# Third layer's input weights: seven forms made in block 0 of stage two instead of in stage one

## The chip, the cores and the metric

One core of a Trainium2 chip. The time is the device time of one execution in microseconds (us); the lower, the better.

## What is computed

Three layers, all in float32. `q`, `k`, `v` are 8 x 8 heads x 576 x 64, `p` is 32 packed queries a head; `moe_w_in` and `moe2_w_in` are 512 x 2048, `moe_w_out` and `moe2_w_out` 2048 x 512 (passed as 64-bit floats and converted on the chip).

```python
def sm_attn(qq, kk, vv):
    s = scale * np.matmul(qq, kk.transpose(0, 1, 3, 2))
    s = s - np.max(s, axis=-1, keepdims=True)
    a = np.exp(s)
    a = a / (np.sum(a, axis=-1, keepdims=True) + 1e-09)
    return np.matmul(a, vv)
p_packed = sm_attn(p, k, v)
x = sm_attn(q, p_packed, p_packed)     # then 4608 tokens x 512
h = x @ moe_w_in;  x = (h * np.cos(h)) @ moe_w_out
h = x @ moe2_w_in
sp = np.where(h > 20.0, h, np.log1p(np.exp(np.minimum(h, 20.0))))
out = (h * np.tanh(sp)) @ moe2_w_out
```

## The kernel before

Every product is made from a high and a low part: a float32 matrix is split into `hi` (a cast on ScalarE) and `lo = x - hi` (a subtraction, mostly on GpSimd), and `mm3` issues three matmuls for one.

**Stage one** makes the attention and the second layer. It runs over n = 0 to 258. Step n issues `l1(n)` (6 matmuls of 288 columns: one of 16 blocks of features for one of 16 tiles of tokens), background work listed for that step, and `l2(n - 3)` (12 matmuls into four accumulators). Between them lies the chain of the step: `chain_first` and `chain_cos` (lines 793 to 803, ScalarE and VectorE) and `chain_split` (line 810 on ScalarE, 813 on GpSimd). The attention of later tiles, the folded weights of the second layer and the third layer's weights are background work, put into the tables `bg_pe`, `bg_ew`, `bg_ld` at given steps. A scheduler that simulates the program fixes each engine's order; each engine then runs its list strictly in that order.

**Stage two** is the third layer, in five blocks of 512, 448, 448, 448 and 448 tokens. Each of its products is done by a seven-product scheme (Strassen's, in Winograd's form) on 2 x 2 blocks. For the first product the weight `moe2_w_in` (`w2i`) is cut into eight units p; each has seven *forms*: its four quadrants, and three sums of them. Per block and p, `product` makes seven products x = 0 to 6 (6 matmuls each), and `sub` puts items of the second product (3 matmuls each) between them. The weight tile of product m is asked for by `ws_load`, five products ahead, since the tag `tmp` has 5 buffers.

**Where the forms come from.** Before, stage one makes all of them. `U_AT` places 16 units at steps 44, 68, ... (`w2i_unit`) and 56, 80, ... (`w2o_unit`, the same for `moe2_w_out`), one each 12 steps. A unit loads two raw tiles of 512 KB (two buffers of tag `raw`), converts them in place (`raw_conv`: lines 548 on ScalarE, 549 and 550 on VectorE), and in the steps +3 to +10 runs the list of `form`: four sums of quadrants on GpSimd (line 569) and seven splits (line 562 on ScalarE, 563 on GpSimd), each followed by a store of 256 KB to memory (line 632 for `w2i`, 598 for `w2o`). Stage two loads each form again in every block (line 532).

All DMAs are issued by SyncE (SP), one queue in order.

Of the kernel before, what the change touches and what calls it, by code (L numbers as in the profile page):

```python
# [8 lines left out]
F32 = mybir.dt.float32  # L9
F32R = mybir.dt.float32r  # L10
I32 = mybir.dt.int32
# [62 lines left out]
T_BUFS = 6  # L74
T_AHEAD = 6
P_AHEAD = 3
U_AT = tuple(44 + 12 * j for j in range(16))
SCALE = 1.0 / math.sqrt(D)
EPS = 1e-9
TWO_PI = 2.0 * math.pi  # L80
# [4 lines left out]
def build(tc, q, k, v, p, w1i, w1o, w2i, w2o, out):  # L85
    nc = tc.nc
    ctx = ExitStack()
    with ctx:
# [6 lines left out]
        def nm(s):  # L95
            cnt[0] += 1
            return f"{s}_{cnt[0]}"
# [422 lines left out]
            return conv(w1o[128 * ft : 128 * ft + 128, :], [128, 512], dst, None)  # L520

        WST = {}

        WS = {}
        NQ = 56 * 5

        def ws_load(m):
            if m >= NQ:
                return
            p, k = divmod(m % 56, 7)  # L530
            w = WS[m] = tp.tile([128, 2, 2, 128], F32R, tag="tmp", bufs=TMP_BUFS, name=nm("ws"))
            nc.sync.dma_start(w.bitcast(F32), WST[(p, K3[k])])

        TST = {}

        def raw_load(raw, parts):
            def f():
                r = tp.tile([128, 512, 2], I32, tag="raw", bufs=2, name=nm("raw"))
                for dst, src in parts(r):
                    nc.sync.dma_start(dst, src)  # L540
                raw.append(r)

            return f
# [32 lines left out]
        def w2o_unit(p):  # L576
            raw = []

            def parts(x):
                def f(r):  # L580
                    src = w2o[256 * p + 128 * x : 256 * p + 128 * x + 128, :].bitcast(I32)
                    for h in range(2):
                        for c in range(2):
                            o = 256 * h + 128 * c
                            yield (
                                r[:, o : o + 128].rearrange("q (a j) t -> q a (j t)", a=4),
                                src[:, 512 * h : 512 * h + 512].rearrange("q (a c y) -> q c a y", a=4, c=2)[:, c],
                            )

                return f  # L590

            def quad(raw, xh):
                x, h = divmod(xh, 2)
                return raw[x][:, 256 * h : 256 * h + 256, 1].bitcast(F32)

            def store(k, w):
                d = TST[(p, k)] = dram.tile([128, 512], F32, name=nm("tst"))
                nc.sync.dma_start(d, w.bitcast(F32).rearrange("p x a f -> p (x a f)"))

            SB = ALU.subtract  # L600
            steps = (
                ((0, 1), None),
                ((2, 2), None),
                (0, 1, 0, SB),
                ((0, 5), None),
                ((3, 3), None),
                (1, 3, 1, SB),
                ((1, 7), None),
                (3, 3, 0, SB),
                ((3, 6), None),  # L610
                (2, 2, 3, SB),
                ((2, 4), None),
            )
            return [raw_load(raw, parts(0)), raw_load(raw, parts(1))], form(raw, quad, store, steps)

        def w2i_unit(p):
            raw = []

            def parts(c):
                def f(r):  # L620
                    src = w2i[256 * c : 256 * c + 256, 256 * p : 256 * p + 256].rearrange("(a p) f -> p a f", p=128)
                    yield r.rearrange("p (a f) t -> p a (f t)", f=256), src.bitcast(I32)

                return f

            def quad(raw, ch):
                c, h = divmod(ch, 2)
                return raw[c].rearrange("p (a f) t -> p a f t", f=256)[:, :, 128 * h : 128 * h + 128, 1].bitcast(F32)

            def store(k, w):  # L630
                d = WST[(p, k)] = dram.tile([128, 2, 2, 128], F32, name=nm("wst"))
                nc.sync.dma_start(d, w.bitcast(F32))

            SB = ALU.subtract
            steps = (
                ((0, 0), None),
                ((2, 1), None),
                (0, 0, 1, SB),
                ((0, 3), None),
                ((3, 4), None),  # L640
                (1, 1, 3, ALU.add),
                ((1, 5), None),
                (3, 3, 0, SB),
                ((3, 2), None),
                (2, 2, 3, SB),
                ((2, 6), None),
            )
            return [raw_load(raw, parts(0)), raw_load(raw, parts(1))], form(raw, quad, store, steps)

# [15 lines left out]
        def at_ew(n, f):  # L665
            bg_ew.setdefault(n, []).append(f)

        def at_ld(n, f):
            bg_ld.setdefault(n, []).append(f)
# [8 lines left out]
        def place(stages, steps, off=0):  # L678
            for (pe, ew), n in zip(stages, steps):
                if off:  # L680
                    pe, ew = pe and hp(pe, off), ew and hp(ew, off)
                if pe is not None:
                    at_pe(n, pe)
                if ew is not None:
                    at_ew(n, ew)
# [52 lines left out]
                at_ew(n, ew)  # L738

        for j, n in enumerate(U_AT):  # L740
            loads, steps = (w2i_unit if j % 2 == 0 else w2o_unit)(j // 2)
            for f in loads:
                at_ld(n, f)
            for i, f in steps:
                at_ew(n + i, f)

        for pair in range(3):
            n0 = 64 * pair
# [16 lines left out]
        for t in range(1, NT):  # L765
            n = Q_N[t - 1]
            loads, stages = q_unit(t)
            at_ld(n - (Q_LD if t > 3 else Q_LD0), after_w(loads))
            place(stages, [n + i for i in (Q_SUB if t > 3 else Q_SUB0)])
        for m in range(TMP_BUFS):  # L770
            at_ld(COMB + 3 + m, lambda m=m: ws_load(m))

        for n in range(PRO - 4, 0):
            run_bg(bg_pe, n)
# [87 lines left out]
        def x_sums(i, a):  # L862
            def f():
                n = N_BLK[i]
                b1, b2 = raws[(i, a)]
                b11, b12, b21, b22 = b1[:, :n], b1[:, n:], b2[:, :n], b2[:, n:]
                t2, t3, t4 = [ld_tile([128, 512])[:, :n] for _ in range(3)]
                nc.vector.tensor_tensor(t3, b22, b12, ALU.subtract)
                nc.vector.tensor_tensor(b12, b12, b11, ALU.subtract)
                nc.vector.tensor_tensor(t2, b22, b12, ALU.subtract)  # L870
                nc.vector.tensor_tensor(t4, b21, t2, ALU.subtract)
                raws[(i, a)] = (b11, b21, t2, t3, t4, b12, b22)

            return f
# [53 lines left out]
        def product(i, p, x, ps, n, first=True):  # L928
            m = 56 * i + 7 * p + x
            w, src = WS.pop(m), X[(i, K3[x])]  # L930
            for a in range(2):
                mm3(ps, w[:, 0, a], w[:, 1, a], src[:, a, 0, :n], src[:, a, 1, :n], first and a == 0, a == 1, not first)
            ws_load(m + TMP_BUFS)

        def split(hl, src, n, eng):
            nc.scalar.copy(hl[:, 0, :n], src)  # L936
# [222 lines left out]
```

## Time and profile before

| | us |
|---|---|
| median of 3 runs | 1581.95 |
| lowest, highest | 1576.72, 1590.94 |
| the profiled execution | 1587.78 |
| its span, first to last instruction | 1585.8 |
| TensorE busy | 1492.7 (94%) |
| VectorE, ScalarE, GpSimd busy | 1093.4, 895.0, 672.3 |

The profile is of one execution, 5.8 us above the median of the runs. A matmul's end is modelled, so "busy" for TensorE hides gaps that are shorter than the modelled overlap of two matmuls. In the names, PE is TensorE, PEld its weight load, DVE VectorE, ACT ScalarE, POOL GpSimd, SP or SPq SyncE and its DMA queue. "acc<-gh,wo" is `l2`, "ps<-aT,wab" `l1`, "ps<-wab,ws" a product of stage two, "acc<-gh,T" an item of its second product.

### The profile page before, as it was taken

What the parts mean: (1) busy time and instruction counts of PE and PEld (TensorE: products, weight loads), DVE (VectorE), ACT (ScalarE), POOL (GpSimd) and SP (SyncE); (2) the same over time, 40 slices, a digit from 0 to 9 for tenths busy, and PEclk for the clock granted to TensorE, in tenths of its full rate; (3) what the DMA queues carried; (4) which work ended last, traced back from release to release, by engine and by line L of the source; (5) the groups of instructions that cost most, each with busy time, mean ns of one, the idle gap of its engine ahead of it and who ended that gap; (6) DMA issues with size and microseconds to landing.
All of it is one profiled execution on the core that took longest, in us unless ns stands there. A gap on an engine that the chain in (4) does not pass through costs nothing.

```text
span 1585.8 us, 28624 instructions
## 1 busy us (share of the span) xinstructions
PE 1492.7 (94%) x9728; PEld 1302.5 (82%) x9728; DVE 1093.4 (69%) x2044; ACT 895.0 (56%) x1844; POOL 672.3 (42%) x682
## 2 busy tenths in 40 slices
PE   3778999999999999998999999999999999999997
PEld 1566778788987898788999888889999899999986
DVE  4885667677766776778764557687567658756656
ACT  3675767677766776766764345435444533543343
POOL 0451346357653665647843025225223521532142
PEclk9889999999999999999999999999999999999999
DMA  9888676557556556543323668788778878777955
GB/s 290 276 214 206 175 186 191 170 146 205 154 158 180 168 163 164 175 123 109 120 68 119 198 197 248 204 231 263 232 214 258 253 213 229 240 215 207 262 150 169
DMA packets 250833, 307.05 MB, mean 194 GB/s; under 512 B 104768, under 2 KB 129856, under 8 KB 250688
## 3 DMA queue, kind: packets, MB, share of 16 engines
q1 hardware_dynamic: 250688, 305.22, 66.6%
q8 instruction: 78, 1.28, 0.3%
q14 instruction: 67, 0.55, 0.1%
HBM read 252.71 MB, written 52.43 MB: 192 GB/s over the span
## 4 chain that ended last, share of the span: by engine, by line
PE 70%; DMA 9%; DVE 7%; ACT 4%; issue 4%; POOL 4%; SPq 1%; DVEq 0%; POOLq 0%; ACTq 0%
PE acc L142 12%; PE acc L143 12%; PE acc L144 12%; PE ps L142 10%; PE ps L143 10%; PE ps L144 10%; PE ps L488 2%; POOL wt L563 2%; DMA raw<-in_moe_w_out_dram 2%; DMA raw<-in_moe_w_in_dram 1%; DVE r L796 1%; DMA kr<-in_k_dram 1%; DVE r L795 1%; DMA kr<-in_q_dram 1%; POOL raw L569 1%
## 5 line engine op out<-in xcount | busy, mean ns | idle before, releaser
L813 POOL TENSOR_TENSOR gh<-r,gh 128x288 fp32r<-128x288 f32 x256 | 216.7, 853 | 286.3 <-ACT gh L810 204.1
L937 POOL TENSOR_TENSOR gh<-t,gh 128x448 fp32r<-128x448 f32 (+1 forms) x120 | 155.2, 1298 | 427.9 <-ACT gh L936 427.9
L143 PE MATMUL acc<-gh,wo 128*128 128x288 f32 x1024 | 301.7, 301 | 1.8 <-POOL gh L813 1.6
L144 PE MATMUL acc<-gh,wo 128*128 128x288 f32 x1024 | 298.2, 298 | 0.0
L142 PE MATMUL acc<-gh,wo 128*128 128x288 f32 x1024 | 276.7, 305 | 6.7 <-ACT gh L810 5.9
L142 PEld LDWEIGHTS acc<-gh,wo 128*128 128x128 f32 x1024 | 182.3, 191 | 41.7 <-issue 16.5
L143 PE MATMUL acc<-gh,T 128*128 128x448 f32 (+1 forms) x560 | 209.6, 374 | 1.3 <-DVE gh L937 1.3
L144 PE MATMUL acc<-gh,T 128*128 128x448 f32 (+1 forms) x560 | 208.9, 374 | 0.0
L143 PE MATMUL ps<-wab,ws 128*128 128x448 f32 (+1 forms) x560 | 208.2, 372 | 0.0
L142 PE MATMUL ps<-wab,ws 128*128 128x448 f32 (+1 forms) x560 | 206.7, 372 | 1.3 <-DMA ws<-wst 1.2
L143 PEld LDWEIGHTS acc<-gh,wo 128*128 128x128 f32 x1024 | 194.1, 190 | 15.8 <-issue 10.1
L144 PE MATMUL ps<-wab,ws 128*128 128x448 f32 (+1 forms) x560 | 206.9, 372 | 0.0
L144 PEld LDWEIGHTS acc<-gh,wo 128*128 128x128 f32 x1024 | 194.2, 190 | 4.1 <-issue 4.0
L937 DVE TENSOR_TENSOR gh<-wo,gh 128x448 fp32r<-128x448 f32 (+1 forms) x160 | 128.8, 810 | 95.4 <-ACT gh L936 94.6
L142 PE MATMUL acc<-gh,T 128*128 128x448 f32 (+1 forms) x560 | 186.5, 375 | 3.2 <-ACT gh L936 3.2
L142 PE MATMUL ps<-aT,wab 128*128 128x288 f32 x512 | 161.1, 315 | 28.2 <-DVE r L803 20.1
L802 ACT ACTIVATE r<-r,halfpi 128x288 f32<-128x288 f32 x256 | 136.2, 535 | 84.4 <-DVE r L796 82.8
L803 DVE TENSOR_TENSOR r<-r,ps 128x288 f32<-128x288 f32 x256 | 114.4, 448 | 69.1 <-ACT r L802 68.1
L143 PE MATMUL ps<-aT,wab 128*128 128x288 f32 x512 | 153.1, 299 | 0.0
L144 PE MATMUL ps<-aT,wab 128*128 128x288 f32 x512 | 152.4, 298 | 0.0
L795 DVE SCALAR_TENSOR_TENSOR r<-ki,ps 128x288 f32<-128x288 int32 x256 | 113.5, 446 | 55.0 <-ACT ki L793 35.7
L793 ACT ACTIVATE ki<-ps,quarter 128x288 int32<-128x288 f32 x256 | 124.0, 495 | 47.5 <-PE ps L144 36.8
(150 smaller groups left out, 2968.5 us busy)
## 6 DMA issues: line engine op xcount, KB each, us to landing
ws<-wst SPq DMA_DIRECT2D x280, 256.0 KB, 3.0
T<-tst SPq DMA_DIRECT2D x280, 256.0 KB, 2.9
kr<-in_k_dram SPq DMA_DIRECT2D x64, 272.0 KB, 5.4
ld<-ws SPq DMA_DIRECT2D x64, 256.0 KB, 3.7
kr<-in_q_dram SPq DMA_DIRECT2D x60, 272.0 KB, 5.3
wst<-wt SPq DMA_DIRECT2D x56, 256.0 KB, 2.7
tst<-wt SPq DMA_DIRECT2D x56, 256.0 KB, 2.2
x2d<-xo SPq DMA_DIRECT2D x64, 144.0 KB, 1.8
```

The costliest lines, as they stand in the source:

```text
L142: nc.tensor.matmul(ps, l0, r0, start=first, stop=False, skip_group_check=more)
L143: nc.tensor.matmul(ps, l0, r1, start=False, stop=False, skip_group_check=more)
L144: nc.tensor.matmul(ps, l1, r0, start=False, stop=last, skip_group_check=more)
L488: return nc.tensor.matmul(st[b][32 * l : 32 * l + 32], PK[(b, g)][r : r + 64, 32 * l : 32 * l + 32], ms[h // 2]["m"][r : r + 64], start=Tr ...
L563: nc.gpsimd.tensor_tensor(lo, src, hi, ALU.subtract)
L569: nc.gpsimd.tensor_tensor(quad(raw, a), quad(raw, b), quad(raw, c), d)
L793: nc.scalar.activation(ki, st["h"], AF.Identity, bias=quarter, scale=1.0 / TWO_PI)
L795: nc.vector.scalar_tensor_tensor(r, ki, -TWO_PI, st["h"], ALU.mult, ALU.add)
L802: nc.scalar.activation(g, g, AF.Sin, bias=halfpi, scale=1.0)
L803: nc.vector.tensor_tensor(g, g, st["h"], ALU.mult)
L813: nc.gpsimd.tensor_tensor(gh[:, 1], st["g"], gh[:, 0], ALU.subtract)
L937: eng.tensor_tensor(hl[:, 1, :n], src, hl[:, 0, :n], ALU.subtract)
```

## The change

`w2i_unit` is gone. `U_AT` now places only the eight `w2o` units, at steps 83 to 220, every 19 or 20 steps. The raw halves of `w2i`, 16 of 512 KB, are placed by `I_AT` at steps 44, 53, 63, 73 and then two behind each `w2o` unit. Each is loaded and converted by `conv` (steps c1 to c3: one operation on ScalarE, two on VectorE, through two `tmp` buffers), and the converted words are stored, 256 KB each, without being summed or split.

In block 0 of stage two, for each unit p: `comb_load` reads the two converted tiles back into two `ld` buffers, `comb_sums` makes the three sums with four operations on VectorE into two more `ld` buffers (of six), and `ws_load` makes each of the 56 weight tiles by a cast on ScalarE and a subtraction on GpSimd, and stores it for blocks 1 to 4. These load the forms as before. The first unit's work and its first five tiles stand in the last steps of stage one (240 to 247). Since `ld` is now in use in block 0, `x_sums` of block 1 writes into buffers of the tags `V` and `o`.

```diff
--- before.py
+++ after.py
@@ -74,7 +74,9 @@
 T_BUFS = 6
 T_AHEAD = 6
 P_AHEAD = 3
-U_AT = tuple(44 + 12 * j for j in range(16))
+U_AT = tuple(83 + 98 * j // 5 for j in range(8))
+I_AT = (44, 53, 63, 73) + tuple(83 + 98 * (j // 2) // 5 + 13 + 3 * (j % 2) for j in range(12))
+I_LAG = 2
 SCALE = 1.0 / math.sqrt(D)
 EPS = 1e-9
 TWO_PI = 2.0 * math.pi
@@ -520,6 +522,30 @@
             return conv(w1o[128 * ft : 128 * ft + 128, :], [128, 512], dst, None)
 
         WST = {}
+        w2s = {}
+
+        def pre2(key, src, shape):
+            return conv(src, shape, None, lambda d: w2s.__setitem__(key, d))
+
+        CB = {}
+
+        def comb_load(p):
+            CB[p] = []
+            for c in range(2):
+                r = ld_tile([128, 512])
+                nc.sync.dma_start(r, w2s[(p, c)])
+                CB[p].append(r.rearrange("p (a f) -> p a f", f=256))
+
+        def comb_sums(p):
+            c0, c1 = CB[p]
+            a11, a21, a12, a22 = c0[:, :, :128], c0[:, :, 128:], c1[:, :, :128], c1[:, :, 128:]
+            u, v = [ld_tile([128, 512]).rearrange("p (x a f) -> p x a f", x=2, a=2) for _ in range(2)]
+            nc.vector.tensor_tensor(u[:, 0], a21, a22, ALU.add)
+            nc.vector.tensor_tensor(u[:, 1], u[:, 0], a11, ALU.subtract)
+            nc.vector.tensor_tensor(v[:, 0], a11, a21, ALU.subtract)
+            nc.vector.tensor_tensor(v[:, 1], a12, u[:, 1], ALU.subtract)
+            CB[p] = (a11, a12, u[:, 1], v[:, 0], a22, u[:, 0], v[:, 1])
+
 
         WS = {}
         NQ = 56 * 5
@@ -529,7 +555,13 @@
                 return
             p, k = divmod(m % 56, 7)
             w = WS[m] = tp.tile([128, 2, 2, 128], F32R, tag="tmp", bufs=TMP_BUFS, name=nm("ws"))
-            nc.sync.dma_start(w.bitcast(F32), WST[(p, K3[k])])
+            if m < 56:
+                nc.scalar.copy(w[:, 0], CB[p][K3[k]])
+                nc.gpsimd.tensor_tensor(w[:, 1], CB[p][K3[k]], w[:, 0], ALU.subtract)
+                d = WST[(p, K3[k])] = dram.tile([128, 2, 2, 128], F32, name=nm("wst"))
+                nc.sync.dma_start(d, w.bitcast(F32))
+            else:
+                nc.sync.dma_start(w.bitcast(F32), WST[(p, K3[k])])
 
         TST = {}
 
@@ -610,40 +642,6 @@
                 ((3, 6), None),
                 (2, 2, 3, SB),
                 ((2, 4), None),
-            )
-            return [raw_load(raw, parts(0)), raw_load(raw, parts(1))], form(raw, quad, store, steps)
-
-        def w2i_unit(p):
...
             return [raw_load(raw, parts(0)), raw_load(raw, parts(1))], form(raw, quad, store, steps)
 
@@ -738,11 +736,18 @@
                 at_ew(n, ew)
 
         for j, n in enumerate(U_AT):
-            loads, steps = (w2i_unit if j % 2 == 0 else w2o_unit)(j // 2)
+            loads, steps = w2o_unit(j)
             for f in loads:
                 at_ld(n, f)
             for i, f in steps:
                 at_ew(n + i, f)
+        for j, n in enumerate(I_AT):
+            w, c = divmod(j, 2)
+            src = w2i[256 * c : 256 * c + 256, 256 * w : 256 * w + 256].rearrange("(a p) f -> p a f", p=128)
+            load, cs = pre2((w, c), src, [128, 2, 256])
+            at_ld(n, load)
+            for i, f in enumerate(cs[:3]):
+                at_ew(n + I_LAG + i // 2, f)
 
         for pair in range(3):
             n0 = 64 * pair
@@ -767,8 +772,11 @@
             loads, stages = q_unit(t)
             at_ld(n - (Q_LD if t > 3 else Q_LD0), after_w(loads))
             place(stages, [n + i for i in (Q_SUB if t > 3 else Q_SUB0)])
+        at_ld(COMB, lambda: comb_load(0))
+        at_ew(COMB + 2, lambda: comb_sums(0))
         for m in range(TMP_BUFS):
-            at_ld(COMB + 3 + m, lambda m=m: ws_load(m))
+            at_ew(COMB + 3 + m, lambda m=m: ws_load(m))
+        at_ld(COMB + 4, lambda: comb_load(1))
 
         for n in range(PRO - 4, 0):
             run_bg(bg_pe, n)
@@ -864,7 +872,12 @@
                 n = N_BLK[i]
                 b1, b2 = raws[(i, a)]
                 b11, b12, b21, b22 = b1[:, :n], b1[:, n:], b2[:, :n], b2[:, n:]
-                t2, t3, t4 = [ld_tile([128, 512])[:, :n] for _ in range(3)]
+                if i == 1:
+                    if a == 0:
+                        raws["t"] = [bt("V", 1024)] + [bt("o", 1024, 2) for _ in range(2)]
+                    t2, t3, t4 = [t[:, 512 * a : 512 * a + n] for t in raws["t"]]
+                else:
+                    t2, t3, t4 = [ld_tile([128, 512])[:, :n] for _ in range(3)]
                 nc.vector.tensor_tensor(t3, b22, b12, ALU.subtract)
                 nc.vector.tensor_tensor(b12, b12, b11, ALU.subtract)
                 nc.vector.tensor_tensor(t2, b22, b12, ALU.subtract)
@@ -930,7 +943,11 @@
             w, src = WS.pop(m), X[(i, K3[x])]
             for a in range(2):
                 mm3(ps, w[:, 0, a], w[:, 1, a], src[:, a, 0, :n], src[:, a, 1, :n], first and a == 0, a == 1, not first)
+            if i == 0 and x == 1 and p < 7:
+                comb_sums(p + 1)
             ws_load(m + TMP_BUFS)
+            if i == 0 and x == 3 and p < 6:
+                comb_load(p + 2)
 
         def split(hl, src, n, eng):
             nc.scalar.copy(hl[:, 0, :n], src)
```

## Rows read from the trace of the kernel before

**Rows 1.** The page, part 1: busy time, share of the span, instructions.

```profile
PE 1492.7 (94%) x9728; PEld 1302.5 (82%) x9728; DVE 1093.4 (69%) x2044; ACT 895.0 (56%) x1844; POOL 672.3 (42%) x682
```

**Rows 2.** Windows: length, busy time of each engine, clock, DMA share, GB/s.

```profile
218.00:250.00 32.00, 32.00 (x307) 30.08 (x300) 21.99 (x58) 23.20 (x55) 18.95 (x23) 0.95 0.68 187
250.00:350.00 100.00, 93.86 (x780) 75.87 (x779) 68.90 (x150) 72.53 (x155) 52.16 (x62) 0.98 0.60 172
350.00:450.00 100.00, 97.48 (x812) 90.13 (x813) 73.24 (x166) 71.17 (x163) 59.34 (x70) 1.00 0.56 159
450.00:550.00 100.00, 96.36 (x826) 77.90 (x822) 71.22 (x159) 72.27 (x159) 57.33 (x69) 1.00 0.67 183
550.00:650.00 100.00, 95.95 (x782) 87.75 (x780) 72.12 (x157) 69.19 (x157) 60.63 (x72) 1.00 0.56 159
650.00:750.00 100.00, 95.79 (x745) 81.03 (x742) 78.45 (x158) 69.17 (x153) 60.54 (x68) 1.00 0.42 136
750.00:857.00 107.00, 104.16 (x780) 102.02 (x780) 73.40 (x154) 72.50 (x159) 66.46 (x74) 1.00 0.26 81
867.00:953.00 86.00, 86.00 (x381) 71.24 (x380) 48.58 (x68) 34.95 (x62) 13.55 (x11) 1.00 0.70 208
```

**Rows 3.** Waits of TensorE, 218 to 857 us: total, times, longest.

```profile
PE ps L142 <- DVE r L803: 10.5, 14, 2.2
PE acc L142 <- ACT gh L810: 5.6, 3, 3.1
...
PE acc L143 <- POOL gh L813: 1.4, 3, 0.6
```

**Rows 4.** Groups of instructions by line and form, whole span.

```profile
L563 POOL TENSOR_TENSOR wt<-raw,wt 128x256 fp32r<-128x256 f32 x112 | 86.7, 790 | 38.0 <-ACT wt L562 33.7 <-DMA kr<-in_k_dram 4.3
...
L569 POOL TENSOR_TENSOR raw<-raw 128x256 f32<-128x256 f32 x32 | 28.7, 896 | 0.3
...
L562 ACT CAST wt<-raw 128x256 fp32r<-128x256 f32 x112 | 44.4, 424 | 8.1 <-POOL raw L569 4.4 <-DVE raw L550 1.7 <-DMA tst<-wt 1.5
...
L550 DVE SCALAR_TENSOR_TENSOR raw<-raw 128x512 int32<-128x512 int32 x32 | 25.0, 782 | 2.3 <-ACT raw L548 1.6
...
L438 DVE SCALAR_TENSOR_TENSOR tmp<-tmp,cvt 128x512 int32<-128x512 int32 x16 | 14.5, 913 | 0.3
```

**Rows 5.** Waits of all engines, 218 to 857 us.

```profile
DVE r L795 <- POOL gh L813: 16.9, 16, 1.7
...
DVE raw L549 <- DMA raw<-in_moe_w_in_dram: 10.2, 9, 2.4
...
ACT raw L548 <- DMA raw<-in_moe_w_in_dram: 5.9, 5, 1.9
```

**Rows 6.** Waits of SyncE's DMA queue, 218 to 857 us.

```profile
SPq L632 <- POOL wt L563: 85.5, 46, 9.6
```

**Rows 7.** Groups by line, 859 to 953 us (block 0).

```profile
L937 POOL TENSOR_TENSOR gh<-t,gh 128x512 fp32r<-128x512 f32 x7 | 9.1, 1294 | 81.2 <-ACT gh L936 81.2
L937 DVE TENSOR_TENSOR gh<-wo,gh 128x512 fp32r<-128x512 f32 x7 | 8.6, 1222 | 2.6 <-ACT gh L936 2.6
...
L1045 DVE TENSOR_TENSOR t<-wo,wo 128x512 f32<-128x512 f32 x7 | 4.8, 691 | 0.6
```

**Rows 8.** Line 796, whole span: count, then min/median/max ns.

```profile
L796 DVE TENSOR_SCALAR r<-r x256: 242/390/1399, 53.0 to 848.2; 128x288 f32<-128x288 f32 x128
```

**Rows 9.** Timeline of ScalarE in block 0: start us, us, instruction.

```profile
868.87 0.59 ACT L1114 COPY m<-ps 128x512 f32<-128x512 f32 x1
```

**Rows 10.** Timeline of TensorE around the same moment.

```profile
868.44 0.39 PE L144 MATMUL ps<-wab,ws 128*128 128x512 f32 x1
...
870.48 0.39 PE L142 MATMUL ps<-wab,ws 128*128 128x512 f32 x1
```

**Rows 11.** The page, part 6: DMA issues, median us to landing.

```profile
ws<-wst SPq DMA_DIRECT2D x280, 256.0 KB, 3.0
...
wst<-wt SPq DMA_DIRECT2D x56, 256.0 KB, 2.7
```

More of the change, by code (lines that the diff above doesn't have):

```diff
@@ L612, in w2o_unit @@
                 ((2, 4), None),
-            )
-            return [raw_load(raw, parts(0)), raw_load(raw, parts(1))], form(raw, quad, store, steps)
-        def w2i_unit(p):
[L617 to L646, printed above, removed]
             )
```

## Prediction

> **What bounds the kernel now.** I read the page's busy shares first: TensorE 94%, GpSimd 42% [rows 1]. That share is an average over two stages, so next come the windows [rows 2], cut at step 44 (218 us, where the first `w2i` unit begins) and at the end of stage one (857 us), with seven of block 0's eight units p in the last row. The reader is to see three things. From 867 to 953 us TensorE has 86.00 of 86 us: block 0 is bound by TensorE alone, with GpSimd busy for 13.55 us. From 218 to 857 us GpSimd is busy for 375.4 of 639 us (the sum of the seven rows), 59%. And in that same stretch TensorE stands idle for only 23.4 us (639 less its seven busy times, 615.6). That is the ceiling of what a relief of stage one can give, 1.5% of the whole, but for gaps too short to show, since a modelled end covers them.
>
> Next I ask who holds TensorE in those 23 us. By its own waits [rows 3], GpSimd is named for 1.4 us only; the PSUM bank that VectorE's line 803 has to free for 10.5 us, in 14 pieces; the cast of line 810 for 5.6 us in three. The lag of three steps between `l1` and `l2` hides most of what GpSimd does late. So the busy 59% is no bottleneck by itself, and I don't expect the 73 us of GpSimd work that leave stage one to come off the time.
>
> **The change, part by part.**
>
> *Removed from stage one.* 56 splits on GpSimd (56 x 0.790 = 44.2 us) and 32 sums there (32 x 0.896 = 28.7 us), 72.9 us together, and 56 casts on ScalarE (56 x 0.424 = 23.7 us) [rows 4]; also 56 stores on SP, whose queue stood for 85.5 us at such stores until GpSimd had finished, with every later load behind them [rows 6]. GpSimd goes from 375 to about 302 us, 47% of the stretch. What TensorE gets of it, by the waits: the 1.4 us on GpSimd directly. Of the 10.5 us on line 803, a part: VectorE waits for GpSimd's line 813 to release a buffer, 16.9 us in 16 pieces [rows 5], and its line 796, which needs 242 ns at best, takes 390 at the median and up to 1399 [rows 8]. I take half, 5 us, as I can't tell which of the 14 waits GpSimd began. Both ends: 0 and 10.5.
>
> A rule of the Trainium skill bears on line 796: SBUF — State Buffer, "Who interferes with whom", says that a VectorE operation with two inputs in SBUF, or one in a two-port mode, and a GpSimd operation that reads SBUF lock each other out for a whole instruction. In this trace the spread of line 796 agrees with that. By the rule alone VectorE's lateness would go with GpSimd's share, 10.5 x 73 / 375 = 2.0 us in place of 5, and the sum below would be 5 us in place of 8.
>
> *What stays in stage one.* 16 conversions, as before: the same operation on ScalarE and two on VectorE, the second 0.913 in this form against 0.782 in place [rows 4], 16 x 0.13 = 2 us more on VectorE, which has 28% free (459 of 639 us busy, [rows 2]); I cost it at nothing, 2 us if that cover is gone. They wait at the head of VectorE's and ScalarE's queues for their raw loads: 10.2 us in 9 pieces and 5.9 us in 5, at most 2.4 [rows 5], and the whole chain of the step is queued behind them. The new placement keeps two steps between a load and its conversion, so these waits can stay; but the loads come singly, and SP has 40 stores fewer ahead of them (56 go, 16 come). Between 0 and 5.9 us gained; I take 1.6, nearer to nothing since the distance is the same. New is that each conversion holds two of the five `tmp` buffers until its store has landed (2.7 us for such a store [rows 11]); the forms held one each, 56 times. Fewer buffers in all (32 against 56), so nothing, if the placing behind the `w2o` units holds; the other case is a rival.
>
> *Added to the tail of stage one.* Steps 240 to 247 get four SP loads, four sums on VectorE and five casts and splits (five times 0.424 and 0.790: 2.1 and 4.0 us). From 750 to 857 us GpSimd is free for 40 us and VectorE for 34 [rows 2], and the first product comes at 859 us. Nothing; at worst the 4.0 us.
>
> *Added to block 0.* For each p: seven casts (3.0 us on ScalarE), seven splits (5.5 us on GpSimd), four sums on VectorE. A sum has 2 x 128 columns; the nearest row, 512 columns from SBUF, takes 0.691 [rows 7], so one takes between half of that and all of it: 1.4 to 2.8 us, and I take 1.6, near the half. A unit p lasts 12.3 us (86 / 7). ScalarE goes from 5.0 to 8.0 us, GpSimd from 1.9 to 7.4, VectorE from 6.9 to 8.5 [rows 2]. All stay under 12.3. The splits are wanted five products ahead: four products of 6 matmuls at 0.226 us (86 / 381) are 5.4 us at least, against 1.2 us for a cast and a split. In `product` a cast now stands ahead of the copy of line 1114, for which the third product waits. In the row shown the last matmul of the first product starts at 868.44, the copy ends at 869.46 and the third product starts at 870.48 [rows 9, 10]: 1.0 us free, and the cast takes 0.42. The cover is the item that the scheduler puts between them; without it (three matmuls, 0.68 us) the room is 0.3 us and each p loses 0.1, 1 us in all. Nothing.
>
> *Moved DMAs.* Block 0 loses 56 loads of 256 KB (3.0 us to landing) and gets 51 stores (2.7 us) and 12 loads [rows 11]; the DMA share of that stretch is 0.70 [rows 2] and rises by about a tenth of that. The loads' consumer is five or more products away. Stores now wait on SP for GpSimd, ahead of the `T` loads, which are six groups ahead. Nothing. `x_sums` in other buffers is the same work.
>
> *The sum.* 1.4 + 5 + 1.6 = 8 us of the profiled execution: 1587.8 - 8 = 1579.8. That execution lies 5.8 us above the median of the runs, and the forecast is of the median: 1582 - 8 = **1574 us**.
>
> **Rivals.**
>
> *All the idle time goes.* If GpSimd is the common cause behind VectorE's and ScalarE's lateness too, the whole 23.4 us go: 1558.5 us. For it: the 85 us of SP waits and line 796's spread. Against it: the longest single wait [rows 3], 3.1 us, is for a cast of ScalarE, not for GpSimd.
>
> *Nothing comes of it.* The lag of three steps hides GpSimd already, and what is late next is VectorE's own work (72% of the stretch): 1582 us. For it: 1.4 us in [rows 3].
>
> *VectorE becomes the bound of block 0 (slower).* Beside GpSimd's split VectorE's line 937 takes 1222 ns; line 1045 takes 691 without it [rows 7]: 0.53 us more. In each p VectorE has four operations with both inputs in SBUF (lines 937, 1045, 1129, one of 992) and gets four sums. If each of the eight waits out a whole split, 0.79, VectorE needs 8.5 + 6.3 = 14.8 us for a p of 12.3, and eight of them make block 0 20 us longer: 1582 - 8 + 20 = 1594 us. It decides from a mean wait of (12.3 - 8.5) / 8 = 0.48 us. Against it: GpSimd would be busy 60% of the time, and an operation that meets a split meets half of one on average: 0.6 x 0.4 = 0.24 us. The lock of the Trainium skill's page named above is the rule by which this would come.
>
> *The conversions hold the step's chain (slower).* A conversion that waits for two `tmp` buffers or for its load blocks ScalarE and VectorE. At the longest wait seen, 2.4 us, 16 of them cost 38 us; at the mean of 10.2 / 9 = 1.1 us they cost 18: 1582 - 8 + 18 = 1592 us.
>
> *The change doesn't do what it says* if the scheduler leaves the moved splits so late that block 0's first products wait: four loads, sums and splits in a row, about 3.0 + 1.6 + 1.2 = 6 us, once: 1580 us. I count it with "nothing comes of it".
>
> **How the numbers follow.** Forecast 0.45 (its own ends are 1564, with all of the 10.5 and the 5.9 us, and 1581); all the idle time goes 0.24; nothing comes of it 0.15; VectorE the bound 0.07; the conversions hold the chain 0.09. The range takes in the second case, with some gaps that the modelled ends hide, and reaches to both slower ones: 1553 to 1594. One per cent, 15.8 us, is about what a measurement of this kernel can tell, its three runs being 14 us apart. Faster by more than that: the second case and an edge of the first, 0.27. Slower: the parts of the two slower cases beyond their prices, and what I don't see, 0.12. Within: 0.61.
>
> **What the profile after should show.** GpSimd about 300 us busy in the stretch from step 44 to the end of stage one, and 7 us for each p of block 0; TensorE idle there some 15 us; block 0's TensorE still full, 12.2 to 12.4 us a p; line 796's median nearer 242; the waits of lines 433 and 434 for raw loads no longer than those of 548 and 549 before. The prediction is wrong if block 0 shows TensorE waiting for a weight tile, for line 1114 or for a bank that VectorE holds; if line 433 waits for a buffer; or if TensorE's idle time in stage one stays at 23 us or falls to nearly nothing.

## The result, and the profile after

The change makes the kernel faster by 1.0%: 1569.64 us median (1563.18 to 1579.15) against 1585.23 (1576.72 to 1590.94), each of 18 runs, a ratio of 0.9901 [0.9884, 0.9917], or 15.6 us. The forecast of 8 us had the sign and half of the size. It started from the 1582 us of three runs, 3 us below the median of 18, so its 1574 us lies nearer to the measured time than its gain does to the measured gain.

The profiled execution of after took 1565.01 us, its span 1562.9 us; before they were 1587.78 and 1585.8. The trace tells where the 22.9 us between the spans came from. The first product of stage two stands in TensorE's timeline, of before and then of after (start, length, instruction):

```profile
859.01 0.39 PE L142 MATMUL ps<-wab,ws 128*128 128x512 f32 x1
```

```profile
843.00 0.40 PE L144 MATMUL ps<-wab,ws 128*128 128x512 f32 x1
```

So 16.0 us are won in stage one, which is the whole of the measured gain. Block 0 then takes 93.83 us before and 93.91 after. Another 6.4 us lie in blocks 3 and 4 (140.0 and 199.3 us before, 136.7 and 196.2 after), which the change doesn't touch. Those belong to the execution and not to the kernel: a second execution of before has 137.2 and 195.8 us there (c0, below).

Stage one after, in the windows of the prediction, shifted to end at the first product (columns as in [rows 2]), and last its block 0 as the window of seven units and as a whole:

```profile
212.00:244.00 32.00, 32.00 (x311) 29.17 (x310) 21.52 (x58) 23.50 (x53) 12.12 (x15) 1.00 0.48 127
244.00:344.00 100.00, 98.22 (x855) 81.26 (x858) 71.98 (x166) 66.73 (x144) 32.56 (x37) 1.00 0.52 135
...
644.00:744.00 100.00, 94.66 (x733) 82.76 (x733) 77.83 (x165) 70.35 (x151) 53.62 (x59) 1.00 0.40 122
744.00:841.00 97.00, 95.26 (x716) 93.16 (x715) 59.02 (x132) 62.12 (x143) 56.85 (x65) 1.00 0.21 69
851.00:937.00 86.00, 85.95 (x381) 71.02 (x380) 65.92 (x95) 49.68 (x109) 54.84 (x58) 1.00 0.70 242
...
843.00:937.00 94.00, 93.95 (x417) 77.64 (x416) 72.13 (x104) 53.90 (x117) 58.10 (x62) 1.00 0.70 242
```

GpSimd has 309.3 us in the seven windows from 212 to 841 us (three of them, with 53.17, 49.46 and 51.52, are not shown), where it had 375.4 [rows 2]; TensorE's idle time there is 18.2 us of 629, where it was 23.4 of 639. That is 5 us less idle time for a gain of 16, so most of the gain isn't seen in these windows.

Two things hide it. First, the windows of the prediction began at 218 us, and part of the change lies ahead of that. From 100 us to the first product both kernels do the same 5934 matmuls (windows of before, then of after; the second and third rows are two short stretches that are needed further on):

```profile
100.00:859.00 759.00, 723.12 (x5934) 631.13 (x5935) 537.89 (x1191) 528.20 (x1159) 412.63 (x476) 0.99 0.56 156
147.00:151.00 4.00, 0.48 (x5) 0.25 (x3) 2.12 (x6) 2.11 (x5) 0.00 (x0) 0.93 1.02 359
151.00:158.00 7.00, 7.00 (x36) 5.02 (x37) 4.55 (x15) 5.06 (x9) 0.79 (x1) 0.55 0.51 118
```

```profile
100.00:843.00 743.00, 715.26 (x5934) 626.21 (x5935) 527.36 (x1192) 506.90 (x1104) 346.70 (x394) 1.00 0.55 147
147.00:151.00 4.00, 3.85 (x34) 2.52 (x34) 2.72 (x12) 3.34 (x7) 0.24 (x1) 1.00 1.04 370
151.00:158.00 7.00, 6.69 (x76) 5.06 (x74) 5.40 (x12) 4.85 (x10) 1.97 (x2) 1.00 1.08 203
```

Second, only 8.1 of these 16 us are idle time (759 - 723.12 = 35.9 before, 743 - 715.26 = 27.7 after). The other 7.9 stand in the busy column: the same matmuls are longer there. From 151 to 158 us TensorE is busy throughout in before, at a granted clock of 0.55, and its matmuls of 288 columns take 0.39 to 0.48 us on the mean, against 0.29 to 0.32 in after. (The counts, 36 and 76, don't compare, as after has many short matmuls there.) This gap cost more than its own length. The second executions agree: 33.8 and 25.2 us of idle time.

**Where in stage one.** The windows can be cut once more, behind the chain's step 88, whose multiplication on VectorE (line 803, in after 811) starts at 373.3 us in before and at 356.4 in after. Before, then after:

```profile
100.00:373.00 273.00, 252.07 (x2180) 209.10 (x2180) 185.88 (x437) 188.25 (x403) 120.67 (x140) 0.97 0.70 184
373.00:859.00 486.00, 471.05 (x3755) 422.03 (x3756) 352.01 (x755) 339.96 (x756) 291.95 (x337) 1.00 0.48 140
```

```profile
100.00:356.00 256.00, 244.73 (x2177) 203.73 (x2177) 179.16 (x431) 176.17 (x373) 90.11 (x101) 0.99 0.68 168
356.00:843.00 487.00, 470.53 (x3758) 422.48 (x3758) 348.20 (x761) 330.73 (x732) 256.60 (x294) 1.00 0.47 135
```

The whole gain, 17 us, is made by step 88 (15.4 in the second executions). The rest of stage one takes 486 us before and 487 after, though GpSimd has 35 us less to do in it.

**Where the gap at 147 us comes from.** The timelines of before around it (start, length, instruction, and in brackets the idle time and what ended it):

```profile
143.89 0.43 ACT L810 CAST gh<-r 128x288 fp32r<-128x288 f32 x1
148.80 0.70 ACT L548 ACTIVATE raw<-raw 128x512 f32<-128x512 f32 x1 [4.48 <-DMA raw<-in_moe_w_in_dram]
...
144.82 0.95 SPq L540 DMA_DIRECT2D raw<-in_moe_w_in_dram  x2
...
148.80 0.43 DVE L549 TENSOR_SCALAR raw<-raw 128x512 int32<-128x512 int32 x1 [4.22 <-DMA raw<-in_moe_w_in_dram]
```

The load is issued at 144.82 us, and its conversions already stand at the head of ScalarE's and VectorE's queues. Both engines stand still for over 4 us until it lands, with the chain of the step behind them, and TensorE runs dry. The program gives this unit to step 44, 218 us; the scheduler has put its conversions beside step 25. That it could do so because an in-place conversion needs no buffer but its own is a reading of the code. The same load and its conversion in after:

```profile
143.99 1.36 SPq L421 DMA_DIRECT2D raw<-in_moe_w_in_dram  x2
...
221.74 0.71 ACT L435 ACTIVATE tmp<-raw 128x512 f32<-128x512 f32 x1
```

Here 78 us lie between the two, and nobody waits. The waits of ScalarE and VectorE for raw tiles, over the same stretch from 100 us, of before and then of after (engine, tile, line, releaser: total, times, longest):

```profile
DVE raw L549 <- DMA raw<-in_moe_w_in_dram: 14.4, 10, 4.2
...
ACT raw L548 <- DMA raw<-in_moe_w_in_dram: 10.4, 6, 4.5
...
ACT raw L548 <- DMA raw<-in_moe_w_out_dram: 8.7, 6, 3.0
...
DVE raw L549 <- DMA raw<-in_moe_w_out_dram: 5.1, 4, 2.3
```

```profile
ACT raw L580 <- DMA raw<-in_moe_w_out_dram: 8.0, 4, 3.2
...
DVE raw L581 <- DMA raw<-in_moe_w_out_dram: 6.3, 4, 2.4
...
ACT tmp L435 <- DMA raw<-in_moe_w_in_dram: 4.7, 6, 2.4
...
DVE cvt L436 <- DMA raw<-in_moe_w_in_dram: 4.6, 3, 3.3
```

38.6 us before, 23.6 after: 15 us less. All of it is in the loads of `w2i` (24.8 to 9.3); those of `w2o` stay (13.8 and 14.3). And nearly all of it lies ahead of the cut at step 88: 22.7 to 8.2 us there, 15.9 and 15.4 behind it, where nothing is gained. That is the theory of the experiments: the gain comes from conversions that stand at the head of two in-order queues. Its rivals: GpSimd's 73 us, which the prediction credited with most of the gain, and the new places of the units in the steps, by which after also has fewer units ahead of step 88.

### The profile page after: what moved, and what is told of

Its sections match the earlier page's. It is cut to its first block, busy times and chain, and to the rows that moved or that the text cites. A ratio compares the mean times of both kernels' runs of the same rounds, so it can differ in the third digit from the quotient of the medians.

```text
span 1562.9 us, 28685 instructions
## 1 busy us (share of the span) xinstructions
PE 1479.3 (95%) x9728; PEld 1297.2 (83%) x9728; DVE 1105.6 (71%) x2076; ACT 888.7 (57%) x1840; POOL 653.6 (42%) x650
## 4 chain that ended last, share of the span: by engine, by line
PE 51%; DVE 5%; ACT 2%; DMA 2%; issue 1%; POOL 1%; SPq 1%; DVEq 0%; ACTq 0%; POOLq 0%
PE acc L144 9%; PE acc L145 9%; PE acc L146 9%; PE ps L144 8%; PE ps L145 8%; PE ps L146 8%; DVE r L804 1%; ACT r L810 1%; DVE r L811 1%; DVE r L803 1%; DMA raw<-in_moe_w_in_dram 1%; DMA tst<-wt 0%; POOL wt L595 0%; DMA kr<-in_q_dram 0%; ACT ki L801 0%
```

## The experiments

Each was run beside runs of before on the same chip, and ratios are to those. "First product" is where stage two begins in the profile of the run (859.0 before, 843.0 after), which shows stage one by itself; a step's start is that of its multiplication on VectorE (line 803 of before); "raw waits" are ScalarE's and VectorE's as above, from 100 us (19.1 and 19.5 before, 12.7 and 10.9 after).

| kernel | ratio to before, 95% | first product | raw waits, ScalarE / VectorE |
|---|---|---|---|
| after | 0.9901 [0.9884, 0.9917] | 843.0 | 12.7 / 10.9 |
| e1, before, first unit's conversions held | 0.9970 [0.9950, 0.9990] | 859.0 | 15.3 / 16.2 |
| e6, before, all conversions held | 0.9865 [0.9835, 0.9895] | 840.7 | 0 / 0 |
| e7, before, forms held and not conversions | 1.0097 [1.0064, 1.0130] | 869.9 | 30.2 / 22.5 |
| e4, before without GpSimd's `w2i` work | 0.9937 [0.9917, 0.9957] | 851.9 | 22.6 / 21.8 |
| e2, after with GpSimd work put back | 0.9897 [0.9867, 0.9926] | 845.6 | 10.0 / 10.5 |
| e3, after at the old places | 0.9886 [0.9859, 0.9913] | 842.1 | 3.6 / 3.5 |
| e9, e3 and conversions held | 0.9911 [0.9877, 0.9945] | 843.4 | 0 / 0 |
| e8, after and conversions held | 0.9818 [0.9780, 0.9856] | 834.2 | 0 / 0 |
| e5, after, block 0's splits twice | 1.0002 [0.9979, 1.0025] | 847.5 | 14.4 / 13.4 |

**Two controls: the kernels before and after, once more (no edit).**

> The kernel before, unchanged, for a second profile. The profile after is 22.9 us shorter than that of before, but 6.4 us of it lie in blocks 3 and 4 of stage two, where the two kernels issue the same work (140.0 and 199.3 us against 136.7 and 196.2). Theory A: that part belongs to the execution (TensorE's pace there), not to the change: this second profile may show blocks 3 and 4 anywhere between 333 and 340 us together, while stage one ends within 2 us of 859. Theory B: it belongs to the program: blocks 3 and 4 again take 339 us within 1 us.

> The changed kernel, unchanged, for a second profile. By theory A (pace of the execution) blocks 3 and 4 may take anything between 333 and 340 us and stage one again ends within 2 us of 843; by theory B (the program) they take 333 us within 1 us again.

They took 1581.99 and 1562.61 us, with the first product at 859.0 and 842.9: in these two pairs stage one repeats to 0.1 us. It doesn't always. e5, below, was run on another chip than these two and has the order of after on every engine up to 760 us; yet its step 216 starts at 746.9 us, where after has 742.4. So a difference of up to some 5 us in stage one between two profiles shows nothing by itself. Block 3 doesn't repeat either. The same window of it in the profiled execution of before and in the second one:

```profile
1236.00:1376.00 140.00, 139.11 (x674) 126.05 (x673) 95.83 (x146) 61.60 (x119) 46.78 (x37) 1.00 0.80 239
```

```profile
1237.00:1374.00 137.00, 136.32 (x673) 125.96 (x672) 96.08 (x146) 61.11 (x118) 46.84 (x36) 1.00 0.80 244
```

The same program needs 3 us less, at a granted clock of 1.00 both times. After has 137.0 us there in its second execution too. Theory A of the two expectations holds. So 6.4 us of the profiles' difference are no gain.

**e1: before, with the first `w2i` unit's conversions held back.** A hold puts them on ScalarE and VectorE behind the chain of a given step; it fixes the order on the engine and adds no wait.

```
+    if STEP[0] < 48:             # in raw_conv
+        for i in CHAIN[42]:
+            es.enter_context(tc.issue_after(i))
...
+    i1 = nc.scalar.activation(g, g, AF.Sin, bias=halfpi, scale=1.0)    # in chain_cos
+    i2 = nc.vector.tensor_tensor(g, g, st["h"], ALU.mult)
+    CHAIN[n] = [getattr(i, "ins", i) for i in (i1, i2)]
```

> The kernel before, with the conversions of the first w2i unit held behind the chain of step 42 on ScalarE and VectorE; its loads, and all GpSimd work, stay. In the trace of before these conversions stand in the queues right behind their load at 145 us, and ScalarE and VectorE wait 4.5 and 4.2 us for it, TensorE 3.8. Theory of the waits (a good part of the gain is conversions that no longer block the step's chain): 4 to 5 us faster, ratio 0.997. Theory of GpSimd's relief: no change within 1 us, as GpSimd's work is the same.

1579.72 us, 4 us faster in the median, but the first product stays at 859.0. By the starts of the steps in the two traces it is 5.0 us ahead of before at step 32, 3.5 at step 48, 2.6 at 72, 1.0 at 144 to 152 and 0.1 from step 232 on. So the gap at 147 us is the wait's, and it isn't worth its 5 us at the end of stage one while the other waits stay. Why it is given back isn't shown, nor where the median's 4 us come from if not from stage one; a ratio this near to 1 says nothing of stage one.

**e2: after, with GpSimd's work put back.** 88 idle operations in a tile of their own, where `w2i`'s forms stood, behind the split of the step's chain:

```
+    def pool_work():
+        with tc.issue_after(LP[0]):     # the last split of the chain
+            nc.gpsimd.tensor_tensor(dummy.rearrange("p (a f) -> p a f", a=2), id2, id2, ALU.subtract)
...
+    for u in range(8):
+        for i in (3, 4, 4, 5, 6, 6, 7, 8, 8, 9, 10):
+            at_ew(44 + 24 * u + i, pool_work)
```

> The changed kernel with 88 idle subtractions of 128 x 256 on GpSimd, from a constant tile into a scratch tile, at the steps of stage one where the w2i units had their 88 operations: the load of GpSimd is as before the change, all else as after. Theory of GpSimd's relief: most of the gain is given back, 8 to 15 us slower than the changed kernel, ratio to before 0.995 to 1.00. Theory of the waits: at most 3 us slower than the changed kernel, ratio to before 0.990 to 0.992. My forecast's terms (1.4 and 5 us by GpSimd) would give 6 us back, 0.994.

The group and the window of the stretch:

```profile
L750 POOL TENSOR_TENSOR dummy<-ident 128x256 f32<-128x256 f32 x88 | 57.3, 651 | 1.6
...
100.00:846.00 746.00, 720.18 (x5936) 628.69 (x5936) 524.87 (x1189) 508.65 (x1104) 402.19 (x480) 0.99 0.54 146
```

GpSimd is back at 402 us (413 before, 347 after), and the ratio is after's. Stage one is 2.6 us longer, which is less than two profiles can differ by. GpSimd's time is worth about that much or nothing, once the rest of the change is in. What this run doesn't put back is waiting: its operations wait for nothing (1.6 us of idle time ahead of them), where the splits of before stood 33.7 us, `w2i` and `w2o` together, for ScalarE's casts [rows 4].

**e4: before, without GpSimd's 88 operations for `w2i`.** The sums and the second halves are left out, and each cast is stored twice, in two DMAs of 128 KB for one of 256 KB, so stage two computes with other weights; all casts and conversions stay.

```
-    nc.gpsimd.tensor_tensor(lo, src, hi, ALU.subtract)
+    if not lite:
+        nc.gpsimd.tensor_tensor(lo, src, hi, ALU.subtract)
...
-    nc.sync.dma_start(d, w.bitcast(F32))
+    for x in range(2):
+        nc.sync.dma_start(d[:, x], w[:, 0].bitcast(F32))
```

> The kernel before without the 88 GpSimd operations of the w2i units: the four sums and the low halves are left out, and each form's cast is stored twice, in two DMAs of 128 KB in place of one of 256 KB (the third layer is computed from wrong weights). Casts, conversions, places and the 56 loads a block stay. Theory of GpSimd's relief: 8 to 15 us faster than before, ratio 0.991 to 0.995. Theory of the waits for loads: within 2 us of before, as the loads and conversions are the same, 0.999 to 1.001; the idle work that came back in the changed kernel cost next to nothing, so I expect this.

```profile
100.00:852.00 752.00, 724.59 (x5935) 629.70 (x5936) 522.87 (x1190) 525.21 (x1156) 340.70 (x388) 0.99 0.57 157
```

Taking GpSimd's work out of before gives 7.1 us of stage one (859.0 to 851.9), and the raw waits don't fall. The expectation of no change is refuted. So GpSimd's work is worth 7 us beside these waits (e4) and 3 or less where there are fewer (e2).

**e6: before, with the conversions of all 16 units held behind the chain of the step for which the program gives them.** All of `w2i`'s forms stay in stage one.

```
+    for i in CHAIN[STEP[0] - 1]:        # in raw_conv, all units
+        es.enter_context(tc.issue_after(i))
```

> The kernel before, with the conversions of all 16 units held, on ScalarE and VectorE, behind the chain of the step at which they stand in the program (2 and 3 steps behind the unit's loads), where the scheduler had put them up to 20 steps earlier, right behind their loads. Theory of the waits: ScalarE's and VectorE's waits for raw tiles (14.6 and 15.3 us from 218 us on, and the 4.5 at 145 us) fall to a third, and the kernel is 8 to 14 us faster than before, ratio 0.991 to 0.995. Rival: the waits were slack, or the units end later and what is lost comes back behind them; ratio 0.998 or more. With the first unit alone held, stage one in the profile gained 5 us at step 32 and had given all of it back at step 240.

```profile
100.00:841.00 741.00, 718.54 (x5936) 630.22 (x5937) 532.21 (x1190) 524.42 (x1156) 412.19 (x476) 0.99 0.58 160
```

1565.41 us, 0.9865: at least as much as the change gives, and more than was expected, with GpSimd at its old 412 us. No wait for a raw tile is left, and TensorE's waits for line 803's banks from 212 us to the end of stage one fall from 10.5 us [rows 3] to 6.6. This run shows that the order of the conversions by itself was worth 18 us of stage one, with GpSimd's work in place. That the change won its 16 us in the same way is then likely, but not shown by it.

**e7: before, with the forms held and the conversions free.** The same hold around the casts, splits and sums, and on GpSimd behind the split of the chain; a hold by itself could have been what helps.

```
+    for i in CHAIN[STEP[0] - 1]:        # in form, around cast, split and sum
+        es.enter_context(tc.issue_after(i))
```

> The kernel before, with the casts, splits and sums of the w2i and w2o units held behind the chain of the step at which they stand in the program; the conversions are free, so that the scheduler puts them right behind their loads, 2 to 4 steps ahead of where the run with held conversions had them. It tells apart what the holding of the conversions did. If it was the waits for raw tiles at the head of ScalarE's and VectorE's queues, they stay here (10 us or more on each) and at most a third of that run's gain comes: ratio 0.994 or more. If it was that the forms no longer run steps ahead of their place, before the step's own chain, the gain comes here too: 0.985 to 0.990.

The waits for raw tiles from 100 us:

```profile
ACT raw L549 <- DMA raw<-in_moe_w_in_dram: 18.1, 11, 3.2
...
DVE raw L550 <- DMA raw<-in_moe_w_in_dram: 17.4, 12, 2.9
ACT raw L549 <- DMA raw<-in_moe_w_out_dram: 12.1, 5, 3.4
DVE raw L550 <- DMA raw<-in_moe_w_out_dram: 5.1, 3, 2.9
```

The raw waits rise from 38.6 to 52.7 us and the kernel is slower, with the first product 10.9 us later. Between e6, before and e7, which have the same instructions but for their order, the waits are 0, 38.6 and 52.7 us and the first product comes at 840.7, 859.0 and 869.9: 0.5 us for each up to before, 0.8 from there on. e7 holds other instructions than e6 does, so its slowdown can't be put down to the raw waits alone.

**e3: after, with the conversions and the `w2o` units at the places that they had before.**

```
-U_AT = tuple(83 + 98 * j // 5 for j in range(8))
+U_AT = tuple(56 + 24 * j for j in range(8))
-I_AT = (44, 53, 63, 73) + ...
+I_AT = tuple(44 + 24 * (j // 2) + j % 2 for j in range(16))
```

> The changed kernel with the old places: w2o units at steps 56, 80, ... 224, every 24, and the two conversions of each w2i unit at 44, 68, ... 212 and one step later, so that the sums and splits still move to block 0 but nothing is placed anew. GpSimd's relief is the same as in the change. If placing is what matters (the units further apart, loads single and behind the w2o units), most of the gain goes: ratio to before 0.995 to 1.00. If it is the work that left stage one on GpSimd, ScalarE and SP, the gain stays: 0.989 to 0.992.

First product at 842.1, ratio 0.9886: the new places give nothing by themselves. In this run the raw waits are only 7.1 us, a third of after's, and the time is no better for it. So the sum of these waits doesn't set the time.

**e8: after, with all conversions held as in e6, and e9: the same at the old places.**

```
-    return [(2, raw_conv(raw, 0)), (3, raw_conv(raw, 1))] + ...
+    return [(2, held(raw_conv(raw, 0))), (3, held(raw_conv(raw, 1)))] + ...
...
-    at_ew(n + I_LAG + i // 2, f)
+    at_ew(n + I_LAG + i // 2, held(f) if i < 2 else f)
```

> The changed kernel with all its conversions held behind the chain of the step at which they stand in the program. If the change gained by conversions that block less, there is left the part of its raw waits that remains (12.7 us on ScalarE, 10.9 on VectorE): 2 to 6 us faster than the change, ratio 0.986 to 0.989. If the two gains are independent, GpSimd's and the conversions', they add: 0.975 to 0.980. If nothing is left, TensorE's own work bounds stage one from here on: 0.990.

> The changed kernel with the old places, and all conversions held: it differs from the kernel before with held conversions only in what the change moves, the sums and splits of w2i. If that move is worth something by itself once no conversion blocks, it is faster than that run (0.9865): 0.980 to 0.984; if not, the same within 2 us, 0.985 to 0.988.

e8 takes 1555.5 us, a ratio of 0.9818 [0.978, 0.9856], the fastest of all and better than both kernels. Its stage one is 24.8 us shorter than before's, about what e6 and e4 gave one by one (18.3 + 7.1 = 25.4). e9 has no raw waits either and takes 1571.92, slower than either expectation: there moving the forms to block 0 gains nothing (843.4, against 840.7 in e6, which keeps them all in stage one at the same places), and neither does taking away the last raw waits (842.1 in e3). Between e8 and e9 only the places differ, and they are worth 9 us of stage one; between after and e3 the same places are worth nothing. I can't say why.

**e5: after, with each split of block 0 made twice.**

```
-    nc.gpsimd.tensor_tensor(w[:, 1], CB[p][K3[k]], w[:, 0], ALU.subtract)
+    for _ in range(2):
+        nc.gpsimd.tensor_tensor(w[:, 1], CB[p][K3[k]], w[:, 0], ALU.subtract)
```

> The changed kernel with each GpSimd split of block 0 made twice. GpSimd's work for a unit p goes from about 7.7 us to 13.8 us, over the 12.3 us that TensorE needs, so if nothing else gives way block 0 is bound by GpSimd: 8 x 1.5 = 12 us slower than the changed kernel, ratio to before about 0.998. If VectorE, locked out by GpSimd, is nearer to the bound than I reckon, it is more: 20 us or over, ratio above 1.002. If block 0 takes it without a change of its 94 us, the five tiles made ahead hide more than I think.

Its block 0, and TensorE's waits in it:

```profile
848.00:955.00 107.00, 98.24 (x413) 75.90 (x412) 84.82 (x105) 53.86 (x117) 101.01 (x110) 1.00 0.61 207
...
PE ps L144 <- DVE u L1010: 3.5, 4, 1.0
PE ps L146 <- POOL ws L561: 2.6, 5, 1.4
```

Block 0 takes 107.9 us, 14 more than after (12 were expected), with GpSimd busy for 101 of 107: GpSimd bounds it now. The cover that hid the moved splits is real and finite. Single, they leave GpSimd busy for 58.10 of 94 us; doubled, there is no room.

## Why the prediction was half right

**The step that failed** is the third term of the sum, the raw loads at the head of the queues. I took 1.6 us, "nearer to nothing since the distance is the same". The distance in the program is the same; the distance on the engines isn't. Converting in place left the scheduler free to put the conversions right behind their loads, 70 us ahead of their step in the case of the first unit. In after they write two `tmp` buffers, and the first stood 78 us behind its load. That the buffers are what holds them is argued from the code, not tried. The raw waits fell by 15 us, all in `w2i`'s loads, and e6 shows that the 38.6 us of before are together worth 18.3 us of stage one. By that rate the 15 us are worth 7, an estimate; my term was 1.6. I had the mechanism in hand and priced it from one side only: the rival "the conversions hold the step's chain" charged 18 us for 16 waits that would appear, while the same waits, there already, were given 1.6.

**The windows began too late.** I cut them at 218 us by the program's step 44. The longest wait, 4.5 us on ScalarE, lies at 144 us, ahead of the window, so [rows 5] shows 2.4 as the longest. The term also took the loads of `w2i` alone: inside the window ScalarE and VectorE waited another 8.7 and 5.1 us, up to 3.0 at a time, for the raw tiles of `w2o`.

**The ceiling wasn't one.** 23.4 us of idle time was to bound the gain. The forecast said "but for gaps too short to show"; in fact half of the gain sits in the busy column. The clock is one part of it: after the gap at 147 us the granted clock was 0.55 over 7 us, near the lower of its levels, 1.2 GHz, where after has 1.00, which is 2.4 GHz. It was the same in the second execution of before (0.53, against 1.00 in that of after). How the rest of the 7.9 us divides isn't settled.

**The terms on GpSimd**, 1.4 and 5 us, 6.4 of the 8, aren't borne out as I put them. TensorE's own waits after, in the prediction's window, were to lose them:

```profile
PE ps L144 <- DVE r L811: 7.7, 12, 1.2
...
PE acc L145 <- POOL gh L821: 1.8, 4, 0.7
...
PE acc L144 <- ACT gh L818: 0.9, 2, 0.6
```

The wait on GpSimd went from 1.4 to 1.8 us; that on VectorE's line from 10.5 to 7.7, and with GpSimd's work put back it is shorter still, 4.9 (e2). What nearly vanished is the wait for ScalarE's cast, 5.6 to 0.9, to which the sum gave no term; it is 0.7 in e6, but also 0.2 in e4. In the time GpSimd's work is worth between 2.6 us or less (e2) and 7.1 (e4). That 8 us came within a factor of two of 15.6 is luck: the third term was too small, and the two others stood for a cause that the waits don't show.

**The checks of stage one** came out close all the same: GpSimd 309 us (forecast about 300), TensorE idle for 18.2 us (some 15). The chain's line 796, now 804, falls from a median of 390 ns to 311, on the way to 242 [rows 8]:

```profile
L804 DVE TENSOR_SCALAR r<-r x256: 251/311/1390, 52.1 to 832.4; 128x288 f32<-128x288 f32 x128
```

That is what the prediction expected from less GpSimd work, and e2 says how little it is worth in time. The waits at lines 433 and 434, now 435 and 436, are shorter than those of 548 and 549, as forecast, and line 435 waits for loads alone, for no buffer. A check that comes true doesn't show that its step carries the time: none of the signs of being wrong came, and the third term was wrong all the same.

**Block 0 is hidden, as forecast.** TensorE is busy for 93.95 of 94 us and shows no wait for a weight tile, for a copy or for a bank. For each p, from the window of 86 us (12.3 us each), VectorE has 9.4 us (forecast 8.5), GpSimd 7.8 (7.4) and ScalarE 7.1 (8.0). VectorE's growth, 17.3 us in that window, is the four sums (17.4 us in block 0); its other lines together did not grow, as line 954 fell by what line 1062 rose. Groups of block 0 after:

```profile
L560 POOL TENSOR_TENSOR ws<-ld,ws 128x256 fp32r<-128x256 f32 x51 | 44.8, 883 | 36.4 <-ACT ws L559 35.1 <-DMA T<-tst 0.6
...
L954 DVE TENSOR_TENSOR gh<-wo,gh 128x512 fp32r<-128x512 f32 x7 | 6.7, 952 | 1.2 <-ACT gh L953 1.2
L1062 DVE TENSOR_TENSOR t<-wo,wo 128x512 f32<-128x512 f32 x7 | 6.6, 940 | 0.2
...
L546 DVE TENSOR_TENSOR ld<-ld,ld 128x256 f32<-128x256 f32 x6 | 5.2, 868 | 0.0
L543 DVE TENSOR_TENSOR ld<-ld,ld 128x256 f32<-128x256 f32 x6 | 5.0, 832 | 4.3 <-DMA ld<-ws 4.3
...
L544 DVE TENSOR_TENSOR ld<-ld,ld 128x256 f32<-128x256 f32 x6 | 4.7, 792 | 0.1
...
L545 DVE TENSOR_TENSOR ld<-ld 128x256 f32<-128x256 f32 x6 | 2.5, 423 | 9.2 <-POOL ws L560 9.2
```

Four sums take 0.832 + 0.792 + 0.423 + 0.868 = 2.9 us, a little above the upper bound of 2.8; I had taken the lower half. Three of them are longer than the 691 ns of a 512-column operation, though half its size; the fourth, at 423 ns, mostly follows a wait for GpSimd's split and starts when that is over.

**The rivals.** "All the idle time goes" has the wrong reason (5 of the 23.4 us went in that stretch); its gain lies as far above the measured 15.6 us as the forecast's 8 lies below. "Nothing comes of it" falls by the interval. "VectorE becomes the bound of block 0" falls: line 1062 (1045 before) went from 691 ns [rows 7] to 940, a quarter of a microsecond for each such operation, as the 0.24 reckoned and short of the 0.48 at which it decides, and line 954 (937 before) fell from 1222 to 952. "The conversions hold the step's chain" is the right mechanism with the wrong sign: the change made those waits fewer.

**What stays open:** why e1's 5 us were given back, why the new places count only with held conversions, why e9 gains nothing on e3 and e6, and how the 16 us divide between waits, GpSimd and the units that the new places moved behind step 88.

## What to carry to other kernels

Look at what stands at the head of each in-order queue when it waits for a DMA, and add up these waits over the whole stage, from the places where the scheduler ran the instructions and not those that the program names. Their sum is a sign and not a price: 38.6 us of them were worth 18 here (e6), and the last 7.1 nothing (e3 and e9). An engine that was busy for 59% gave 7 us at most when it was relieved; two engines that waited a few microseconds at a time ahead of the chain gave 18, for an ordering alone. Cut the gain by where it is made: here it was over by step 88. And the idle time of the bounding engine was no ceiling here, since what followed a gap ran slower and counted as busy.

## What the runs showed of the hardware

- After TensorE had been busy for only 0.48 of 4 us (147 to 151 us in before), its granted clock over the next 7 us was 0.55, and a matmul of 288 columns took 0.39 to 0.48 us on the mean, against 0.29 to 0.32 in the same stretch of after at 1.00. In the second execution of before it was 0.81 of 4 us, and 0.53 behind it.
- At a granted clock of 1.00, matmuls of 448 columns follow each other in block 3 at 0.207 us (the median) in one execution of before and 0.203 in the other, 140.0 us against 137.2 for the block. The trace shows no cause.
- Beside GpSimd's splits a 512-column sum of VectorE with both inputs in SBUF takes 940 ns on the mean, against 691 in before, where none of the seven meets a GpSimd operation, and 256-column sums take 792 to 868, where the one that follows a split's end takes 423. The Trainium skill, SBUF — State Buffer, "Who interferes with whom", says that such operations of the two engines exclude each other for a whole instruction; the numbers agree, and the price was hidden here. VectorE's line 796, with one such input, took 309 ns at the median and 314 at most in the 78 of its 256 runs in before that met no GpSimd operation, and 535 at the median in the others.
